# The output of a token tile written in two DMAs instead of one

## The chip, the cores and the metric

The kernel runs on one core of a Trainium2 chip. The metric is the device time of one execution in microseconds (us), as the median of several runs. The core has five instruction queues that matter here: PE (TensorE, matrix multiplications, with the loading of weights shown apart as PEld), DVE (VectorE), ACT (ScalarE), POOL (GpSimd) and SP (SyncE), which in this kernel issues every DMA.

## The reference

Four sequences of 768 tokens, eight heads of 48 elements, so a model width of 384. A delta-rule attention (a serial recurrence over the tokens) is followed by a gated mixer with a causal convolution and by a gated MLP that mixes over tokens:

```python
# attention, per batch and head
k_n = k / (norm(k) + 1e-6)
for t in range(S):
    y[t] = q[t] @ state
    state = state + beta[t] * outer(k_n[t], v[t] - k_n[t] @ state)
# first block
gate = sigmoid(causal_conv5(x, conv_w)); val = x @ w_val
x = (gate * val) @ w_out
# second block
h = gelu_tanh(x @ w_in); u, v = h[..., :512], h[..., 512:]
v_n = (v - mean(v)) / sqrt(var(v) + 1e-6) * g_ln
v_s = w_sg @ v_n + b_sg            # over tokens, 768 x 768
return x + (u * v_s) @ w_out2
```

## The kernel before

The recurrence is worked through in chunks of 64 tokens, 12 per sequence and 48 in all (`seq`, `attend`), with matrices prepared ahead for pairs of chunks (`keys`, `gram`, `base`, `merge`). Its result goes to a DRAM buffer. The two blocks behind it are worked through in token tiles of 256, three per sequence and twelve in all, each in six steps: `front` (load x, convolution, gate), `value`, `hidden`, `gates`, `mix` and `final`. The tiles of one sequence run beside the recurrence of the next; behind the last chunk only tile work is left. Matrices are split into two halves of 16 bits, and each product takes three matmuls (`mm3`).

`final` makes the output of a tile, 384 features by 256 tokens, as three blocks of 128 features. They are taken in two groups, `m0 = 0` with two blocks and `m0 = 2` with one; each group has a PSUM buffer of its own from a ring of three (`bank`). A group's matmuls (nine with `wo` and twelve with `w2` for each block) end in one ACT copy into the tile `o`, of 128x512 or 128x256 elements. Before the change, one DMA then writes the whole of `o` to DRAM (line 998). `o` shares a ring of two buffers (tag `a`) with the tile `a` of `front`, so a `front` that gets its buffer waits until the output DMA has read it.

No instruction is issued when its line runs. Each call is put on record by `Program.add`; `in_order` then lays all of them out in one list with a planner: it gives each operation a planned cost, and a priority that is the weighted cost of the longest chain of operations behind it, divided by the longest chain of all, plus a constant for some stages (lines 119 to 126). The weight of a DMA is 1.949, and its planned time contains its bytes / 250,000 per us. Each engine gets its instructions in the order of the planned times and works through them in that order; SP's list of DMAs is one of these. The planner also lets SP hold when eight DMAs have not landed.

Of the kernel before, what the change touches and what calls it, by code (L numbers as in the profile page):

```python
# [346 lines left out]
def kernel(  # L347
# [17 lines left out]
    nc = Program(tc)  # L365
    P, B, NC, PR, E = kn_in.shape
# [8 lines left out]
    TT = 256  # L375
# [93 lines left out]
    def mm3(ps, a, b, start, stop):  # L469
        for i, (x, y) in enumerate(((0, 0), (0, 1), (1, 0))):  # L470
            nc.tensor.matmul(out=ps, lhsT=a[x], rhs=b[y], start=start and i == 0, stop=stop and i == 2)
# [379 lines left out]
    def wsl(nm, k, cols):  # L851
        return wt[nm][:, 0, k, cols], wt[nm][:, 1, k, cols]
# [5 lines left out]
    def bank():  # L858
        return ps_m.tile([P, 2, TT], F32, name="ps_mlp", tag="m")

    def pairs(n):
        return [(i, min(2, n - i)) for i in range(0, n, 2)]
# [121 lines left out]
    def final(b, tt):  # L984
        gvh = kept.pop(("gv", b, tt))
        gts = [kept.pop(("gt", b, tt, d0)) for d0, _ in pairs(KF)]
        o = mp.tile([P, KD, TT], F32, name="o", tag="a", bufs=2)
        for m0, n in pairs(KD):
            ps = bank()
            for m in range(n):  # L990
                cols = slice((m0 + m) * 128, (m0 + m + 1) * 128)
                for k in range(KD):
                    mm3(ps[:, m], wsl("wo", k, cols), (gvh[:, 0, k], gvh[:, 1, k]), k == 0, False)
                for d in range(KF):
                    mm3(ps[:, m], wsl("w2", d, cols), (gts[d // 2][:, 0, d % 2], gts[d // 2][:, 1, d % 2]),
                        False, d == KF - 1)
            nc.scalar.activation(out=o[:, m0:m0 + n], in_=ps[:, 0:n], func=AF.Copy, scale=1.0 / (SGT * SW2))
        nc.sync.dma_start(out=out[b].rearrange("(k p) t -> p k t", p=P)[:, :, tt * TT:(tt + 1) * TT], in_=o)

# [3 lines left out]
    def add_order(add):  # L1005
        for tt in range(NTT):
            for f in (front, value, hidden):
                add(f, 0, tt)
        for b in range(B):
            nx = b + 1 if b + 1 < B else None  # L1010

            def nxt(f, tt):
                if nx is not None:
                    add(f, nx, tt)

            last = NTT - 1
            nxt(front, 0)
            for tt in range(NTT):
                add(gates, b, tt)
                if tt == 0:  # L1020
                    nxt(value, 0)
                else:
                    add(final, b, tt - 1)
                add(mix, b, tt, 0)
                if tt == 1:
                    nxt(hidden, 0)
                add(mix, b, tt, 2)
            nxt(front, 1)
            nxt(value, 1)
            add(final, b, last)  # L1030
            nxt(front, 2)
            nxt(value, 2)
            nxt(hidden, 1)
            nxt(hidden, 2)
# [96 lines left out]
```

## Time and profile before

| | |
|---|---|
| median of 3 runs | 700.64 us (699.04 to 838.62) |
| profiled execution | 701.2 us |
| its span, first to last instruction | 699.5 us |
| mean granted TensorE clock | 0.912 |
| instructions | 22,383 |
| bytes moved by DMA | 94.42 MB |

The profile is of one execution. Its span is the time from the first to the last instruction on the core; the profiled execution took 1.7 us longer than that. Busy times are sums over instructions of an engine. A granted clock of 1.00 is TensorE at full speed.

### The profile page before, as it was taken

What the parts mean: (1) busy time and instruction counts of PE and PEld (TensorE: products, weight loads), DVE (VectorE), ACT (ScalarE), POOL (GpSimd) and SP (SyncE); (2) the same over time, 40 slices, a digit from 0 to 9 for tenths busy, and PEclk for the clock granted to TensorE, in tenths of its full rate; (3) what the DMA queues carried; (4) which work ended last, traced back from release to release, by engine and by line L of the source; (5) the groups of instructions that cost most, each with busy time, mean ns of one, the idle gap of its engine ahead of it and who ended that gap; (6) DMA issues with size and microseconds to landing.
All of it is one profiled execution on the core that took longest, in us unless ns stands there. A gap on an engine that the chain in (4) does not pass through costs nothing.

```text
span 699.5 us, 22383 instructions
## 1 busy us (share of the span) xinstructions
PE 555.3 (79%) x9183; PEld 459.1 (66%) x9183; DVE 563.7 (81%) x1536; ACT 377.5 (54%) x857; POOL 195.3 (28%) x189
## 2 busy tenths in 40 slices
PE   0615736656696498899989998899999999998897
PEld 0503315645575377688778867797977887776786
DVE  8899999997787889989998999899979746563321
ACT  5644646656567756686455767344667533433111
POOL 4625350246214462433402322002412100102000
PEclk9999866655599599999999999999999999999999
DMA  6643405897788968599668964677674754210121
GB/s 203 165 136 126 147 11 125 181 197 142 150 177 166 238 140 173 111 187 252 137 117 178 235 132 85 144 127 156 147 158 89 150 98 111 86 48 1 53 76 46
DMA packets 327639, 94.42 MB, mean 135 GB/s; under 512 B 274545, under 2 KB 316913, under 8 KB 327537
## 3 DMA queue, kind: packets, MB, share of 16 engines
q1 hardware_dynamic: 327536, 93.00, 59.9%
q8 instruction: 72, 1.18, 0.7%
q14 instruction: 31, 0.25, 0.1%
HBM read 51.81 MB, written 23.33 MB: 107 GB/s over the span
## 4 chain that ended last, share of the span: by engine, by line
DVE 37%; PE 26%; DMA 15%; ACT 10%; issue 6%; SPq 3%; POOL 2%; POOLq 0%; ACTq 0%; DVEq 0%
PE ps_mlp L109 20%; DVE X L109 5%; DVE tmp L109 4%; DVE wst L109 3%; SPq L109 3%; DVE a L109 3%; DMA wg<-wgd 2%; PE ps_y L109 2%; ACT v L109 2%; DVE ps_mlp L109 2%; DMA ws<-wh 2%; DMA m1p<-gx 2%; DVE wh L109 2%; DMA kf<-in_kn 2%; DMA bs<-in_b_sg 2%
## 5 line engine op out<-in xcount | busy, mean ns | idle before, releaser
L109 PE MATMUL ps_mlp<-wg,vnh 128*128 128x256 f16 x864 | 104.5, 273 | 5.6 <-DVE ps_mlp L109 1.6
L109 PEld LDWEIGHTS <-kj 112*128 112x128 f16 (+1 forms) x1632 | 75.3, 101 | 38.1 <-issue 29.0
L109 PEld LDWEIGHTS <-vnh 128*128 128x128 f16 x864 | 82.4, 98 | 19.4 <-issue 3.7
L109 PEld LDWEIGHTS <-kc 64*64 64x64 f16 x1920 | 47.0, 130 | 56.0 <-DVE kc L109 21.7
L109 DVE TENSOR_TENSOR X<-X,tmp 128x30 f32<-128x30 f32 (+9 forms) x180 | 67.5, 375 | 1.7
L109 DVE TENSOR_TENSOR tmp<-X 128x30 f32<-128x30 f32 (+9 forms) x180 | 65.6, 365 | 1.7
L109 PE MATMUL ps_mlp<-gth,w 128*128 128x256 f16 x432 | 60.2, 272 | 0.0
L109 PE MATMUL ps_mlp<-gvh,wi 128*128 128x256 f16 x432 | 57.8, 276 | 2.1 <-ACT u L109 1.1
L109 PE MATMUL ps_mlp<-wi,gvh 128*128 128x512 f16 x216 | 57.6, 379 | 1.9 <-ACT a L109 1.1
L109 PEld LDWEIGHTS <-ws 112*128 112x128 f16 (+1 forms) x1104 | 48.5, 102 | 14.0 <-issue 10.7
L109 PEld LDWEIGHTS <-m1p 128*128 128x128 f16 x1152 | 45.6, 99 | 17.5 <-issue 12.8
L109 DVE SCALAR_TENSOR_TENSOR ps_mlp<-ps_mlp,gl,bs 128x256 f32<-128x256 f32 x48 | 22.7, 488 | 41.8 <-PE ps_mlp L109 41.4
L109 DVE SCALAR_TENSOR_TENSOR a<-x,cw,a 128x256 f32<-128x256 f32 x108 | 54.4, 543 | 0.6 <-ACT a L109 0.5
L109 POOL TENSOR_TENSOR vnh<-v,vnh 128x512 f16<-128x512 f32 x24 | 28.0, 1182 | 89.0 <-ACT vnh L109 89.0
L109 PE MATMUL ps_mlp<-gvh,wo 128*128 128x256 f16 x324 | 49.0, 274 | 4.8 <-ACT u L109 3.0
L109 PE MATMUL ps_mlp<-xh,wv 128*128 128x256 f16 x324 | 51.2, 272 | 0.3 <-ACT o L109 0.3
L109 PEld LDWEIGHTS <-wo 128*128 128x128 f16 x342 | 31.6, 100 | 26.8 <-ACT wo L109 11.1
L109 PE MATMUL ps_y<-mh,ws 128*128 128x64 f16 x576 | 45.7, 199 | 4.4 <-DMA ws<-wh 3.0
L109 PE MATMUL pk<-i,kc 64*64 64x64 f16 x704 | 23.0, 216 | 32.8 <-DVE kc L109 19.4
L109 PE MATMUL ps_y<-qh,ws 112*128 112x64 f16 x528 | 42.7, 198 | 5.4 <-DVE mh L109 5.0
L109 PEld LDWEIGHTS <-wi 128*128 128x128 f16 x432 | 41.0, 98 | 8.3 <-issue 2.8
L109 POOL TENSOR_TENSOR xh<-x,xh 128x780 f16<-128x780 f32 x12 | 20.3, 1690 | 85.4 <-ACT xh L109 81.8
(148 smaller groups left out, 1391.4 us busy)
## 6 DMA issues: line engine op xcount, KB each, us to landing
keys_d<-kc SPq DMA_DIRECT2D x22, 512.0 KB, 4.5
ws<-wh SPq DMA_DIRECT2D x88, 128.0 KB, 3.8
kj<-keys_d SPq DMA_DIRECT2D x44, 256.0 KB, 4.5
wg<-wgd SPq DMA_DIRECT2D x12, 768.0 KB, 5.7
qf<-in_qt SPq DMA_DIRECT2D x24, 224.0 KB, 4.0
kf<-in_kn SPq DMA_DIRECT2D x12, 384.0 KB, 4.4
vf<-in_vn SPq DMA_DIRECT2D x24, 192.0 KB, 3.9
xd<-ys SPq DMA_DIRECT2D x48, 96.0 KB, 2.7
```

Of the source, the lines that this page charges most:

```text
L109: op.call()
```

## The change

The DMA moves into the loop over the two groups. Each group's copy is followed by a DMA of its part of `o`: 256 KB for `m0 = 0`, 128 KB for `m0 = 2`. Everything else in the source stays.

```diff
@@ def final(b, tt):
             nc.scalar.activation(out=o[:, m0:m0 + n], in_=ps[:, 0:n], func=AF.Copy, scale=1.0 / (SGT * SW2))
-        nc.sync.dma_start(out=out[b].rearrange("(k p) t -> p k t", p=P)[:, :, tt * TT:(tt + 1) * TT], in_=o)
+            nc.sync.dma_start(out=out[b].rearrange("(k p) t -> p k t", p=P)[:, m0:m0 + n, tt * TT:(tt + 1) * TT],
+                              in_=o[:, m0:m0 + n])
```

## Rows read from the trace of the kernel before

**Rows 1.** The page: engine, busy us, share of the span, instructions.

```profile
PE 555.3 (79%) x9183; PEld 459.1 (66%) x9183; DVE 563.7 (81%) x1536; ACT 377.5 (54%) x857; POOL 195.3 (28%) x189
```

**Rows 2.** Busy time by stage: stretch, its length, then engines, clock, DMA share.

```profile
0.00:327.00 327.00, 209.10 (x4287) 168.57 (x4288) 293.05 (x777) 201.95 (x460) 132.89 (x142) 0.82 0.69 160
327.00:555.00 228.00, 215.15 (x3535) 181.21 (x3533) 207.11 (x594) 131.00 (x304) 52.32 (x39) 1.00 0.71 141
555.00:611.00 56.00, 53.67 (x729) 46.63 (x726) 31.97 (x86) 22.77 (x54) 3.94 (x3) 1.00 0.45 103
611.00:643.00 32.00, 28.75 (x216) 20.72 (x216) 17.34 (x57) 13.25 (x25) 6.19 (x5) 1.00 0.12 37
643.00:668.30 25.30, 22.41 (x188) 19.14 (x188) 7.28 (x14) 3.37 (x6) 0.00 (x0) 0.93 0.13 37
668.30:673.70 5.40, 4.62 (x42) 3.75 (x41) 1.88 (x3) 1.97 (x4) 0.00 (x0) 1.00 0.74 214
673.70:695.20 21.50, 21.50 (x196) 19.07 (x196) 5.05 (x9) 2.30 (x6) 0.00 (x0) 1.00 0.08 27
695.20:699.50 4.30, 0.10 (x1) 0.00 (x0) 0.00 (x0) 0.84 (x2) 0.00 (x0) 0.92 0.26 91
```

**Rows 3.** The page: the chain that ended last, by engine.

```profile
DVE 37%; PE 26%; DMA 15%; ACT 10%; issue 6%; SPq 3%; POOL 2%; POOLq 0%; ACTq 0%; DVEq 0%
```

**Rows 4.** Groups by line and form: count, busy us, mean ns, idle before.

```profile
L109 ACT ACTIVATE o<-ps_mlp 128x512 f32<-128x512 f32 x12 | 7.1, 593 | 22.9 <-PE ps_mlp L109 22.9
L109 ACT ACTIVATE o<-ps_mlp 128x256 f32<-128x256 f32 x12 | 4.5, 378 | 3.4 <-PE ps_mlp L109 3.4
```

**Rows 5.** DMA issues: count, KB each, median us from issue to landing.

```profile
xd<-ys SPq DMA_DIRECT2D x48, 96.0 KB, 2.7
out_x<-o SPq DMA_DIRECT2D x12, 384.0 KB, 3.0
```

**Rows 6.** Timeline of ACT, one tile's two copies: start us, us, instruction.

```profile
395.48 0.37 ACT L109 ACTIVATE o<-ps_mlp 128x256 f32<-128x256 f32 x1
...
408.50 0.60 ACT L109 ACTIVATE o<-ps_mlp 128x512 f32<-128x512 f32 x1 [0.16 <-PE ps_mlp L109]
```

**Rows 7.** The chain that ended last, its last pieces: start us, us, what.

```profile
695.17 0.60 ACT o L109
695.77 0.28 ACTq L1127
```

**Rows 8.** Timeline of all engines at the end of the span.

```profile
695.17 0.87 ACT L109 ACTIVATE o<-ps_mlp 128x512 f32<-128x512 f32 x2 [5.44 <-PE ps_mlp L109]
696.07 0.37 SPq L109 DMA_DIRECT2D out_x<-o  x1
```

**Rows 9.** DMA from 690 to 700 us, 40 slices, and the last issue.

```profile
GB/s 336 360 352 262 4 0 0 0 0 0 0 0 0 0 0 0 0 0 0 0 0 0 0 0 0 0 0 29 328 352 336 356 172 0 0 0 0 0 0 0
...
out_x<-o SPq DMA_DIRECT2D x1, 384.0 KB, 2.5
```

**Rows 10.** Timeline of SP's queue around the output at 409 us.

```profile
409.12 0.40 SPq L109 DMA_DIRECT2D out_x<-o  x1
409.99 2.85 SPq L109 DMA_DIRECT2D tbd<-tah  x3
412.94 1.82 SPq L109 DMA_DIRECT2D kj<-keys_d  x2
```

**Rows 11.** The chain that ended last, seen from the stretch 300 to 420 us.

```profile
409.12 4.07 DMA out_x<-o
```

**Rows 12.** Waits from 405 to 420 us: total us, times, longest.

```profile
ACT a L109 <- DMA out_x<-o: 0.4, 1, 0.4
```

**Rows 13.** Waits of SP's queue from 327 to 555 us.

```profile
SPq L109 <- ACT o L109: 3.0, 1, 3.0
```

## The prediction

> **What bounds the kernel now.** I began with the busy shares [rows 1]: PE and DVE are busy for 79% and 81% of the span, so neither bounds all of it, and the span has to be cut into stages. The stage table [rows 2] does that. Up to 327 us DVE is busy for 293.05 of 327 us at a mean granted clock of 0.82; no tile's output is written there. From 327 to 555 us PE (215.15 of 228) and DVE (207.11 of 228) are both nearly full and the DMA engines are busy for 0.71 of the time: recurrence, matrices of the next set and the token tiles run side by side. From 555 us on PE is what counts: 53.67 of 56, 28.75 of 32, 22.41 of 25.3, 4.62 of 5.4 and 21.5 of 21.5 us. The last 4.3 us hold almost no PE work: they are the last copy and the last output DMA. The chain of waits [rows 3] says the same by engine: DVE 37%, PE 26%, DMA 15%, and SP's queue, into which the new DMAs go, only 3%.
>
> The output path itself: twelve tiles, each with one copy of 128x512 (593 ns) and one of 128x256 (378 ns) [rows 4] and one DMA of 384 KB that lands after a median of 3.0 us [rows 5]. The two copies of a tile are not always neighbours. In one tile the narrow one starts at 395.48 and the wide one at 408.50 us [rows 6]; the list puts whichever matmuls it likes first. In the last tile they are neighbours: the chain's end shows the wide copy at 695.17 for 0.60 us and then the other [rows 7], the two together take 0.87 us and the DMA is issued at 696.07 [rows 8].
>
> **The change part by part.** It removes twelve DMAs of 384 KB and adds twelve of 256 KB and twelve of 128 KB; no byte, matmul or copy is added. I make the sum against the profiled execution, 701.2 us (span 699.5 plus 1.7 around it), which lies 0.56 us above the median of 700.64.
>
> *The tail.* In the last tile, 1.15 us of the DMA's time is data: the DMA slices [rows 9] are full from about 696.75 on, at 328 to 356 GB/s, mean 343, and 393,216 bytes / 343 GB/s = 1.15 us; it lands 2.5 us after its issue. Half sizes: 256 KB take 0.76, 128 KB take 0.38 us. What is gained depends on which half ends last. (a) If the copies stay together as now, the first half is issued at 695.80, the second 0.40 us later (one issue is 372 to 400 ns, rows 8 and 10), at 696.20; with the same 0.68 us from issue to data as now, the data ends at 696.48 + 1.15 = 697.63 in place of 697.90: 0.27 us gained. (b) If the list finishes the wide group first, the wide copy and its DMA lie beside the narrow group's matmuls; after PE's end come only the narrow copy (0.38 for 0.87, 0.49 gained) and 128 KB of data (0.76 gained): 1.25 us. (c) If the wide group ends last, 0.27 + 0.39 = 0.66. The worst is a second issue that is 0.13 us later than today's single one with nothing gained in the data. I take (b), -1.25, since the list's priorities contain the size of the DMA behind an operation: by lines 119 to 122 a 256 KB DMA is worth 1.949 x 131,072 / 250,000 = 1.02 more than a 128 KB one, some twelve matmuls of priority, and so the wide group goes ahead. Bounds -1.25 to +0.13.
>
> The Trainium skill (DMA: Bandwidth & Descriptors, Anatomy of one DMA) gives a DMA of the gpsimd path about 2.0 us plus bytes / 436 GB/s; by that figure the data term of (b) would be 0.60 in place of 0.76, an estimate that leaves the sum within 0.2 us.
>
> *The buffer behind it.* o and front's a share a ring of two buffers, so a later front waits until the output has been read. That wait shows once: the chain of a middle stretch runs through the output DMA that was issued at 409.12 and took 4.07 us [rows 11], and ACT lost 0.4 us to it [rows 12]. With the last DMA smaller the buffer can come free earlier, by at most the 0.4 that was lost: 0 to -0.4, I take -0.2. Then ACT is held by DVE, as before.
>
> *SP's time.* Twelve more issues at the 0.40 us of [rows 10]: 4.8 us of SP, six of them beside the recurrence (2.4 us). An issue costs something only if the transfer queued behind it is awaited; SP's queue is 3% of the chain [rows 3], so I take +0.5 between 0.1 (3% of 4.8, rounded) and 4.8. After 585 us nothing hurries behind it; before, the cover is SP's spare time, and without it all 4.8 would show.
>
> *The added wait on SP.* SP works through its list in order, so the first half's issue waits for its copy with everything behind it. Between 327 and 555 us SP waited once for a copy of o, 3.0 us [rows 13], in six output DMAs (the tiles of the first two sequences): queued behind were the pieces of tbd and the kj of the next step [rows 10], for which the recurrence's matmuls wait. Six new such issues: one more wait of that kind is likely, and as kj is fetched ahead I let 0.5 of 3.0 through; bounds 0 and 3.0.
>
> *The new order.* This is the largest term, and the one that no row of before shows. The whole program is one list, laid out by a planner from its own costs. The new operations move planned times from the first output on, and sizes change the weighted chains; where the longest one ends in the last output, all priorities are rescaled by a thousandth or so and ties flip from the start. So I expect the instructions of all engines in another order in many places, with the same work. What that can win is PE's uncovered time in the stretches behind the recurrence, 611 to 673.7 us, where PE alone decides and another filling can help: 3.25 + 2.89 + 0.78 = 6.92 us [rows 2]. Before that a hole of PE lies beside a nearly full DVE and I don't count on filling it. What it can lose is of the size of what a mixed stretch loses today, 12.85 us in 327 to 555 [rows 2]. Between -6.92 and +12.85 the middle is +3.0, and I take that; no row favours one end.
>
> Sum: 701.2 - 1.25 - 0.2 + 0.5 + 0.5 + 3.0 = 703.75 in the profile's terms, less 0.56 against the median: 703.2 us, 0.4% over before.
>
> **The rivals.** *Slower: outputs block SP's list.* If the first halves are planned where ACT really comes late, each of the six in the busy stretch holds SP as at 409 us: 3.0 + 0.40 = 3.4 us, and what is held is tbd, kj and ws, on which the serial recurrence waits. Six times 3.4 is 20.4 us: 700.6 + 20.4 = 721. It decides from the fifth that passes whole (17 us, 2.4%). For it: DMA is 15% of the chain, SP's queue is packed back to back around the outputs [rows 10]. Against: only one of the six present outputs was waited for there, and kj is fetched a step ahead. Chance 0.11, with the part of the order term that goes beyond its bound.
>
> *Faster: the new order fills PE's holes.* All of PE's uncovered time from 327 to 695.2 us is 12.85 + 2.33 + 3.25 + 2.89 + 0.78 = 22.1 us; to pass 2% it would have to fill 14 of them, with the tail 13. Time about 686. Against: PE's holes before 611 us lie beside a DVE that is busy for over nine tenths up to 555. Chance 0.02.
>
> *Every DMA pays its fixed time.* If the part of a transfer that doesn't depend on its size stood on the path, the twelve added DMAs would cost twelve times the 2.7 us that a 96 KB DMA takes to land [rows 5]: 32 us, 733. Against: SP goes on to the next issue 0.87 us after the output's at 409.12 [rows 10], long before its landing at 413.2, and nobody but a late front waits for an output. Chance 0.01. The Trainium skill (the same page, Rules for kernel authors) speaks for this rival: it wants many small transfers coalesced into one large one. The rows of 96 KB and 384 KB, 2.7 and 3.0 us, agree that size matters little to landing; they don't show that landing is on the path.
>
> *The change does nothing but split.* If the order stays, the time is 700.6 with 0.3 to 1.3 us off: 699.4 to 700.4, inside the forecast's range. Chance 0.08, since the planner uses the sizes.
>
> **How the numbers follow.** A measurement of this kernel can tell about 2%, 14 us, from no change. The forecast (0.78) and the bare split (0.08) lie within it, 0.86; slower by over 2% are the first rival and the third, 0.12; faster has 0.02. For the range, all terms at their low ends give 700.64 - 1.25 - 0.4 + 0.1 - 6.92 = 691.8. Upwards, the order term at its end gives 703.2 + 9.85 = 713; with the other costs half way to their ends (2.1 and 1.2) 716.4. All ends at once (721) is the slower rival, which I leave out: 692 to 716.
>
> **What would show it.** Twelve output DMAs of 256 and twelve of 128 KB, issued at about 0.4 us each, one right behind each copy. At the end: a wide copy that starts over 1 us before PE's end, one narrow copy after it, and some 0.5 us less from PE's end to the last issue. No row in the waits in which SP holds for a copy of o longer than 3 us before 555 us. If another wait (wg, kj, X) has grown in the chain while the bytes and busy times stay as they are, it is the order. The prediction is wrong if the two traces have the same order of instructions (then less than 700.6), or if the recurrence's stretch up to 585 us has grown by over 10 us behind SP's waits.

## The result: one per cent slower

Median 707.34 us (703.53 to 713.44) against 700.66 before; the ratio is 1.0101, with a 95% interval of 1.0055 to 1.0148. That is inside the 2% that the prediction called no change and inside its range of 692 to 716, but it is clear of noise, and the cause was open: the prediction had put +3.0 us on the new order and +1.0 on SP. A ratio, here and below, is worked out from the single executions, the few slow ones left out, and need not be the quotient of the two medians.

The page of the changed kernel (the profiled execution took 706.63 us), busy shares and chain by engine, against [rows 1] and [rows 3]:

```profile
span 704.8 us, 22396 instructions
...
PE 560.8 (80%) x9183; PEld 462.3 (66%) x9183; DVE 567.7 (81%) x1536; ACT 378.4 (54%) x857; POOL 194.6 (28%) x189
...
DVE 32%; PE 32%; DMA 12%; ACT 8%; issue 7%; SPq 6%; POOL 3%; POOLq 0%; ACTq 0%; DVEq 0%
```

The counts of PE, DVE, ACT and POOL are those of before: no work was added. PE is busy for 5.5 us longer with the same 9,183 matmuls, so some of them ran slower; SP's queue has gone from 3% to 6% of the chain, which looks like the prediction's first rival. Its output DMAs stand against those of [rows 5]: two thirds and one third of the bytes land after a median of 2.3 and 2.4 us, where the whole took 3.0.

```profile
out_x<-o SPq DMA_DIRECT2D x12, 256.0 KB, 2.3
...
out_x<-o SPq DMA_DIRECT2D x12, 128.0 KB, 2.4
```

The stage table shows where the time went. Its borders are the issues of the same `wg` load in both kernels (to about a microsecond), so each row holds about the same work. First the changed kernel, then the kernel before; columns as in [rows 2]:

```profile
327.00:474.00 147.00, 138.42 (x2378) 116.85 (x2376) 141.34 (x403) 83.09 (x196) 31.78 (x25) 1.00 0.69 140
474.00:565.00 91.00, 83.39 (x1219) 68.45 (x1216) 71.31 (x200) 49.33 (x112) 19.79 (x14) 0.96 0.65 127
565.00:616.00 51.00, 50.26 (x667) 43.70 (x665) 28.05 (x76) 21.33 (x49) 3.93 (x3) 1.00 0.44 106
616.00:704.80 88.80, 77.54 (x656) 63.40 (x654) 33.97 (x86) 22.93 (x42) 6.20 (x5) 1.00 0.17 50
```

```profile
327.00:474.00 147.00, 137.12 (x2367) 116.00 (x2365) 137.56 (x398) 83.32 (x197) 31.39 (x25) 1.00 0.71 143
474.00:555.00 81.00, 78.02 (x1171) 65.21 (x1168) 69.55 (x197) 47.68 (x108) 20.93 (x14) 1.00 0.70 136
555.00:608.50 53.50, 52.13 (x717) 45.41 (x714) 29.55 (x81) 21.58 (x52) 3.94 (x3) 1.00 0.45 105
608.50:699.50 91.00, 78.92 (x654) 63.90 (x651) 33.96 (x86) 22.92 (x42) 6.19 (x5) 0.98 0.16 49
```

Up to 474 us nothing is lost. The next stretch takes 91 us in place of 81, with a PE clock of 0.96 in place of 1.00. Behind it 2.5 and 2.2 us come back. The instruction lists agree: PE's list is the same up to its 4,667th matmul, at about 351 us, and from there it differs in some 1,900 places; the first difference in SP's list is the first output, at 344 us.

Inside that stretch, the recurrence's copy of its state on ACT marks each chunk. Two neighbouring ones, changed kernel first:

```profile
482.07 0.33 ACT L109 ACTIVATE wh<-ps_state 112x192 f16<-112x192 f32 x1 [3.03 <-PE ps_state L109]
...
499.36 0.33 ACT L109 ACTIVATE wh<-ps_state 112x192 f16<-112x192 f32 x1 [1.34 <-PE ps_state L109]
```

```profile
481.15 0.33 ACT L109 ACTIVATE wh<-ps_state 112x192 f16<-112x192 f32 x1 [2.67 <-PE ps_state L109]
...
492.88 0.35 ACT L109 ACTIVATE wh<-ps_state 112x192 f16<-112x192 f32 x1
```

17.3 us in place of 11.7: 5.6 us in one chunk. The changed kernel's copies of the state are 0.9 us late ahead of this chunk, 6.5 us behind it, 4.2 and 2.2 at the next two, and 8.2 at the third. That third copy stands behind a cast on ACT that waits for its load, a second place at which time is lost:

```profile
535.21 0.85 ACT L109 ACTIVATE xh<-x 128x780 f16<-128x780 f32 x1 [2.76 <-DMA x<-xd]
```

Here are DVE, then POOL, then PE of the changed kernel in the chunk of 17.3 us:

```profile
481.64 0.20 DVE L109 TENSOR_TENSOR X<-X,tmp 128x30 f32<-128x30 f32 x1
481.75 4.31 DVE L109 SCALAR_TENSOR_TENSOR a<-x,cw,a 128x256 f32<-128x256 f32 x4
485.98 0.48 DVE L109 SCALAR_TENSOR_TENSOR ps_mlp<-ps_mlp,gl,bs 128x256 f32<-128x256 f32 x1
```

```profile
481.92 1.43 POOL L109 TENSOR_SCALAR_AFFINE_SELECT X<-X 128x1024 f32<-128x1024 f32 x1 [18.48 <-DVE X L109]
483.41 0.16 POOL L109 MEMSET X<- 128x32 f32 x1
483.65 2.12 POOL L109 TENSOR_TENSOR X<-X,bt 128x1024 f32<-128x1024 f32 x1
```

```profile
486.51 4.00 PE L109 MATMUL ps_mlp<-wg,vnh 128*128 128x256 f16 x18 [3.80 <-DVE ps_mlp L109]
```

And the same place in the kernel before:

```profile
483.08 0.20 DVE L109 TENSOR_TENSOR X<-X,tmp 128x30 f32<-128x30 f32 x1
483.19 0.42 DVE L109 SCALAR_TENSOR_TENSOR qh<-qf,qh 112x256 f16<-112x256 f32 x1
483.52 1.67 DVE L109 SCALAR_TENSOR_TENSOR a<-x,cw,a 128x256 f32<-128x256 f32 x4
```

```profile
483.36 2.96 POOL L109 TENSOR_SCALAR_AFFINE_SELECT X<-X 128x1024 f32<-128x1024 f32 x1 [27.36 <-DVE X L109]
```

```profile
482.86 2.12 PE L109 MATMUL ps_mlp<-wg,vnh 128*128 128x256 f16 x18 [1.13 <-DVE ps_mlp L109]
```

Read it from DVE. Four convolution steps of a later tile take 4.31 us in the new list and 1.67 in the old, and POOL's work on X starts beside them in both. In the new list DVE is held up, in the old one POOL is (2.96 for 1.43). Behind the four stands the mix's step, for which PE waits 3.80 us. PE then works at half speed: its next 18 matmuls take 4.00 us in place of 2.12. The stage table of the changed kernel around that stop gives the clock:

```profile
481.00:482.50 1.50, 1.46 (x34) 1.25 (x33) 1.50 (x6) 0.43 (x2) 0.58 (x1) 1.00 0.74 117
482.50:486.50 4.00, 0.21 (x1) 0.00 (x0) 4.00 (x5) 0.50 (x2) 3.13 (x3) 0.90 1.04 218
486.50:493.00 6.50, 6.49 (x37) 3.94 (x37) 4.31 (x12) 1.09 (x3) 0.00 (x0) 0.54 0.43 71
493.00:500.00 7.00, 7.00 (x107) 6.40 (x106) 5.67 (x13) 5.00 (x8) 2.74 (x1) 1.00 0.17 57
```

The granted clock is 1.00 before the stop and 0.54 in the 6.5 us behind it, so near the lower of its two levels (1.2 of 2.4 GHz); from 493 us it is back. The kernel before keeps 1.00 in all four stretches.

So there were two theories to tell apart. *Order*: the DMAs cost nothing, the re-laid list does. *Issue or wait*: SP's added issues, or its added waits for a copy, cost the time.

### The profile page after: what moved, and what is told of

Its sections match the earlier page's. It is cut to its first block, busy times and chain, and to the rows that moved or that the text cites. A ratio compares the mean times of both kernels' runs of the same rounds, so it can differ in the third digit from the quotient of the medians.

```text
span 704.8 us, 22396 instructions
## 1 busy us (share of the span) xinstructions
PE 560.8 (80%) x9183; PEld 462.3 (66%) x9183; DVE 567.7 (81%) x1536; ACT 378.4 (54%) x857; POOL 194.6 (28%) x189
## 3 DMA queue, kind: packets, MB, share of 16 engines
q8 instruction: 72, 1.18, 0.7%
## 4 chain that ended last, share of the span: by engine, by line
DVE 32%; PE 32%; DMA 12%; ACT 8%; issue 7%; SPq 6%; POOL 3%; POOLq 0%; ACTq 0%; DVEq 0%
PE ps_mlp L109 24%; SPq L109 6%; DVE X L109 4%; DVE a L109 4%; PE ps_y L109 3%; DVE tmp L109 3%; DVE wst L109 3%; DVE ps_mlp L109 2%; DMA bs<-in_b_sg 2%; DMA x<-xd 2%; PE ps_q L109 2%; DMA wg<-wgd 2%; ACT v L109 2%; DMA wst<-in_w_out 2%; DVE wh L109 1%
## 5 line engine op out<-in xcount | busy, mean ns | idle before, releaser
L109 PE MATMUL ps_mlp<-wg,vnh 128*128 128x256 f16 x864 | 106.4, 276 | 12.8 <-DVE ps_mlp L109 6.5
L109 PEld LDWEIGHTS <-kj 112*128 112x128 f16 (+1 forms) x1632 | 77.2, 102 | 38.0 <-issue 28.7
L109 PE MATMUL ps_mlp<-gvh,wi 128*128 128x256 f16 x432 | 56.0, 272 | 3.0 <-ACT v L109 1.6
L109 DVE SCALAR_TENSOR_TENSOR a<-x,cw,a 128x256 f32<-128x256 f32 x108 | 56.5, 570 | 1.5 <-ACT a L109 1.4
L109 PE MATMUL ps_mlp<-gvh,wo 128*128 128x256 f16 x324 | 45.7, 272 | 4.6 <-ACT u L109 2.6
```

The lines of the kernel that those rows point to most:

```text
L109: op.call()
```

## The experiments

All ratios are to the kernel before on the same chip, with a 95% interval.

| kernel | what differs | median us | ratio |
|---|---|---|---|
| e1 | old list, two DMAs at the old place | 703.66 | 1.0040 [1.0013, 1.0067] |
| e2 | new list, one DMA | 710.00 | 1.0108 [1.0066, 1.0149] |
| e3 | old list, each half behind its copy | 701.49 | 1.0009 [0.9979, 1.0039] |
| e4 | old list, six DMAs | 708.32 | 1.0112 [1.0070, 1.0153] |
| e5 | new list, convolution steps moved | 701.20 | 1.0016 [0.9996, 1.0036] |
| e6 | new list, cast moved | 708.04 | 1.0113 [1.0086, 1.0141] |
| e7 | new list, both moved | 702.42 | 1.0008 [0.9983, 1.0032] |
| e8 | last tile alone in two DMAs | 699.44 | 0.9982 [0.9950, 1.0014] |
| e9 | new list, mix's step moved alone | 705.64 | 1.0066 [1.0032, 1.0099] |
| e10 | old list, one query step moved | 703.98 | 1.0054 [1.0024, 1.0084] |
| n1 | another list, one DMA | 701.89 | 1.0007 [0.9978, 1.0037] |
| n3 | another list, one DMA | 706.19 | 1.0065 [1.0035, 1.0095] |

**Lists and DMAs apart (e1 to e4).** The planner can be shown one thing and the chip given another: an operation goes on record with the sizes that the planner is to see, and its call issues what is wanted.

```diff
 # e1: the planner sees one DMA; its call issues two
-        nc.sync.dma_start(out=dst, in_=o)
+        def parts():
+            for part in (slice(0, 2), slice(2, 3)):
+                tc.nc.sync.dma_start(out=dst[:, part], in_=o[:, part])
+        nc.add("sync", "dma_start", parts, dict(out=dst, in_=o))
 # e2: the planner sees two; the later call issues the whole
+            nc.add("sync", "dma_start", partial(whole, dst, o, seen), dict(out=dst[:, m0:m0 + n], in_=o[:, m0:m0 + n]))
 # e3, in trace(): the first half goes out once its copy is planned to end, the second at the old place
             for op in ops:
+                while early and early[0][0] <= op.start:
+                    early.pop(0)[2]()
                 op.call()
 # e4: as e1, one block of features and half the tokens at a time
+            for k in range(KD):
+                for h in range(2):
```

> The planner sees the one DMA of before, so all engines keep the list of before; only at the place of the output DMA in SP's list two DMAs (256 and 128 KB) are issued one behind the other. Theory 'order' (the 1% comes from the new list of instructions, not from the DMAs): 699 to 702 us, no change. Rival 'issue' (the twelve more issues on SP cost the time): 705 to 709 us.

> The planner sees the two DMAs of the changed kernel, so PE, DVE, ACT and POOL have the lists of the changed kernel; but one DMA of 384 KB is issued, at the place of the later of the two, and nothing at the other. Theory 'order': 705 to 709 us, 0.6 to 1.3% over before, though the output is written as before. Rivals 'issue' and 'wait' (the cost lies in the added DMAs or in SP's added waits): 699 to 702 us.

> The list of before on PE, DVE, ACT and POOL; of SP's list only the output DMAs change: each half is issued behind its own copy, the first as soon as its copy is planned to be done, the second at the old place. This is the change without its new order. Theory 'order': 699 to 702 us. Rival 'wait' (SP's new holds for the first copy delay tbd, kj and ws): 704 to 710 us, with more time of SP spent in waits for copies of o before 555 us.

> The list of before, with six DMAs of 64 KB (one block of features, half the tokens each, rows of 512 bytes) at the place of each output DMA: 60 more issues than before. Doubles the cost of 'issue' fivefold: at 6.7 us for twelve it expects 730 to 735 us, and 24 us more of SP's time. Theory 'order': under 705 us, only what 30 more issues beside the recurrence let through.

The pair that decides is e2 and e3. The changed kernel's list without its DMAs (e2) costs 1.08%, as much as the change; its DMAs without its list (e3) cost 0.09%, not to be told from nothing. In e3 SP waited for a copy of o once between 327 and 555 us, for 1.0 us, less than before [rows 13]:

```profile
SPq L115 <- ACT o L116: 1.0, 1, 1.0
```

So *wait* falls. *Issue* has a small part: e4's 60 added DMAs cost 1.12% of 700.35, 7.8 us or 0.13 us each, so twelve would cost 1.6 us at that rate; what of it is the issue and what the smaller transfer was not told apart. In "doubles the cost fivefold" the expectation counts 60 against 12. e4 missed the under 705 that *order* had expected, by 3 us, and was over 21 us below what *issue* had. e1 stays unclear: 0.4% is more than its twelve issues give by e4's price, and in its profiled execution, the slowest of its twelve, the state's copy that before starts at 304.66 us starts at 307.79, so 3.1 us of its excess lie ahead of the first output, where the lists are the same.

**Which part of the list (e5 to e7, e9).** The changed kernel, with single operations moved in the finished list; in each move no operation is carried past one that needs it.

```diff
 # in trace(), on the changed kernel's list
         ops = self.in_order()
+        ops = self.move(ops, convs, last)   # e5: the four steps behind the mix's, the state's and tbd's step
+        ops = self.move(ops, [cast], wh)    # e6: the cast xh behind the copy of the state
+        # e7: both moves;  e9: ops = self.move(ops, convs, mix), behind the mix's step alone
```

> The changed kernel with one edit of its list: four of DVE's convolution steps, which in its trace take 4.31 us beside POOL's work on X at 482 us while the mix's step and the recurrence's step stand behind them, are moved behind those steps. Theory 'two places' (the new list loses its time at two places, this one and the cast at 532 us): chunk 16 of the recurrence comes 3 to 6 us earlier, 702 to 705 us in all. Rival 'spread' (these places only show a loss that sits in the whole list): no change, 706 to 709 us.

> The changed kernel with another edit of its list: one ACT cast (xh of the first tile of the last sequence), which in its trace waits for its load of x while the recurrence's copy of the state stands behind it for some 2.8 us, is moved behind that copy. Theory 'two places': the state's copy comes 3 to 6 us earlier, 702 to 705 us in all. Rival 'spread': 706 to 709 us.

> Both moves of the two kernels above in the changed kernel's list. Theory 'two places': the loss is gone and the gain of the last tile is left, 698 to 702 us. Rival 'spread': 705 us and more.

> The changed kernel with the four convolution steps moved behind the mix's DVE step alone; they still stand ahead of the recurrence's steps (the state's copy and tbd). Theory 'PE's stop' (the loss is PE standing still for 3.8 us behind the mix's step and then running at half its clock): most of it is gone, 700 to 703 us. Rival 'recurrence' (the loss is the recurrence's DVE step that stands behind the four): 705 to 709 us.

e5 takes the loss away with four DVE steps moved by six places: 1.0016, with 1 in its interval, some 0.8% below the changed kernel and lower than either theory had. e6 takes none (1.0113, as its rival *spread* had): in its trace the cast no longer stands ahead of the state's copy and that chunk is 2.5 us shorter, the next one is 0.8 longer, and over its six executions nothing is gained. e7 is e5 again, 0.4 us above what *two places* had. So *two places* falls; one decides. By the state's copies e5 is 4.7 us ahead of the kernel before at 518 us and level with it at 540: the new list wins and loses time at other places too, and without this one they come out even. The rows of e5, DVE, POOL and PE, at that place:

```profile
480.42 0.48 DVE L137 SCALAR_TENSOR_TENSOR ps_mlp<-ps_mlp,gl,bs 128x256 f32<-128x256 f32 x1
...
482.42 2.02 DVE L137 SCALAR_TENSOR_TENSOR a<-x,cw,a 128x256 f32<-128x256 f32 x5
```

```profile
482.15 4.07 POOL L137 TENSOR_TENSOR X<-X,bt 128x1024 f32<-128x1024 f32 x1
```

```profile
481.21 2.13 PE L137 MATMUL ps_mlp<-wg,vnh 128*128 128x256 f16 x18
```

The steps now take 0.40 us each, POOL is held up (4.07 us for 2.12), PE waits for nothing and keeps its clock. e9 asks what share each half of the harm has. There the mix's step goes ahead, and nothing else:

```profile
484.10 0.48 DVE L147 SCALAR_TENSOR_TENSOR ps_mlp<-ps_mlp,gl,bs 128x256 f32<-128x256 f32 x1
484.49 4.14 DVE L147 SCALAR_TENSOR_TENSOR a<-x,cw,a 128x256 f32<-128x256 f32 x4
488.55 0.68 DVE L147 BATCH_NORM_STATS2 st<-v 128x6 f32<-128x512 f32 x1
489.15 0.34 DVE L147 SCALAR_TENSOR_TENSOR wh<-ps_state,wh 112x192 f16<-112x192 f32 x1
```

```profile
484.89 2.13 PE L147 MATMUL ps_mlp<-wg,vnh 128*128 128x256 f16 x18
...
489.54 0.26 PE L147 MATMUL ps_q<-wh,kj 112*128 112x48 f16 x4 [2.32 <-DVE wh L147]
```

The mix's 18 matmuls are neither held nor slowed. PE stops later, for 2.32 us, until the recurrence's step is done, and its granted clock stays at 1.00. Yet 1.0066 is left, inside what the rival *recurrence* had: the four steps still take 4.14 us and the recurrence's step on its state stands behind them. By the points of the ratios the mix's stop and the slow clock are worth 0.35% (1.0101 to 1.0066) and the recurrence's hold 0.50% (1.0066 to e5's 1.0016). The intervals of e9 and of the changed kernel overlap, so the first share is not shown to differ from nothing. The traces have it the other way round: the chunk takes 17.3 us in the changed kernel, 13.2 in e9 and 10.8 in e5. How the loss divides stays open.

**The harm put into the old list (e10).** One operation moved, PE's, ACT's, POOL's and SP's lists as before.

```diff
-X<-X,tmp   qh<-qf,qh   a x4   ps_mlp     (DVE's list before)
+qh<-qf,qh   X<-X,tmp   a x4   ps_mlp
```

> The list of before with one DVE step (the query's lower half, qh) moved ahead of the last step on X, so that the four convolution steps follow X at once, as in the changed kernel. Theory 'pairing' (which of DVE and POOL holds the other up is decided by what stands on DVE when POOL's work on X begins): the four take about 4.3 us in place of 1.67, and the time grows by 1 to 4 us, 702 to 705. Rival: they stay at 1.7 us and the time is that of before, 699 to 702.

```profile
483.84 0.20 DVE L124 TENSOR_TENSOR X<-X,tmp 128x30 f32<-128x30 f32 x1
483.96 4.30 DVE L124 SCALAR_TENSOR_TENSOR a<-x,cw,a 128x256 f32<-128x256 f32 x4
488.18 0.48 DVE L124 SCALAR_TENSOR_TENSOR ps_mlp<-ps_mlp,gl,bs 128x256 f32<-128x256 f32 x1
```

```profile
484.12 1.44 POOL L124 TENSOR_SCALAR_AFFINE_SELECT X<-X 128x1024 f32<-128x1024 f32 x1 [28.88 <-DVE X L124]
```

4.30 us in place of 1.67, as *pairing* had it, and 0.54% of time; the chunk takes 14.3 us in place of 11.7. The pairing is shown from both sides: taken out of the new list the loss goes, put into the old one a loss comes. The traces of e2 and e6, which keep the new list here, have 4.30 us too. In e10 the mix's first step stands ahead of the four and its matmuls are not slowed (2.13 us); what comes later is the mix's second step and the recurrence's.

The Trainium skill (SBUF — State Buffer, SBUF: two separate sides) says that DVE and GpSimd have a pair of ports in common, held for a whole instruction by whichever starts first, also by a DVE operation with two SBUF inputs against a GpSimd operation that reads SBUF, and that the other stands still. The convolution step and the query's step have two such inputs, and the rows agree that one of the two engines is held up at each meeting. Singly, the four steps of the changed kernel take 0.47, 1.47, 0.47 and 2.13 us. The two long ones:

```profile
482.14 1.47 DVE L109 SCALAR_TENSOR_TENSOR a<-x,cw,a 128x256 f32<-128x256 f32 x1
...
483.93 2.13 DVE L109 SCALAR_TENSOR_TENSOR a<-x,cw,a 128x256 f32<-128x256 f32 x1
```

The first ends about 0.3 us behind POOL's select, the second about 0.3 us behind POOL's addition (`X<-X,bt`), so DVE stood still for one POOL instruction each time and got a step through between the two. In the old list it isn't a matter of one instruction: all four steps take 0.48 us, and POOL's select, 2.96 us long, ends 1.1 us behind the last of them. Nor do the starts in the trace decide: e5's POOL addition is shown from 482.15, 0.27 us ahead of its first step, and is held all the same. Why POOL gets in between two DVE steps in one list and not in the other is not shown by these runs.

The planner reckons with such a hold (`held` in `in_order`): a POOL operation that comes while DVE has a step with two SBUF inputs waits until DVE's string of them is over. So in both of its plans the four steps run through and POOL's select waits behind them. The chip did that in the old list and not in the new one.

**The tail alone (e8), and two other lists (n1, n3).**

```diff
 # e8, in final's loop; all other tiles keep their one DMA
+            if (b, tt) == (B - 1, NTT - 1):
+                nc.sync.dma_start(... m0:m0 + n ..., in_=o[:, m0:m0 + n])
 # n1, n3: one DMA per tile; only the planner's cost of issuing it grows, by 0.3 and 0.6 us
-    return 0.68 if onchip or n > 4 * row else 0.48, move, False
+    more = 0.3 if out.tensor.name == "out_x" else 0.0
+    return (0.68 if onchip or n > 4 * row else 0.48) + more, move, False
```

> Only the last of the twelve tiles is written in two DMAs, and the planner knows it; the lists of ACT, DVE and POOL are those of before, PE's differs in a few ties and in the last tile, SP's in the last DMA. The prediction's tail term (b): 1.25 us less, 698.5 to 700 us, with one narrow copy and 128 KB after the last matmul. Rival: the copies stay together and at most 0.3 us is gained, or the ties of PE cost it, 700 to 703 us.

> Another list from the same kernel as before: one output DMA per tile as before, only the planner's cost of issuing it is 0.3 us higher, which changes some 1,900 places of PE's list and none of the work. Its DVE list has no convolution steps between the last step on X and the mix's step. Theory 'place' (only a list with that pairing loses): 698 to 703 us. Rival 'any other list loses': 704 to 710 us.

> As the kernel with 0.3 us, with 0.6 us: a third list, in which single convolution steps stand among others behind the last step on X. Theory 'place': 698 to 704 us. Rival 'any other list loses': 704 to 710 us.

e8's ratio of 0.9982 has 1 in its interval: its point is the prediction's tail term (0.0018 x 701 = 1.3 us), but the measurement can't confirm it. Its ratio is the lowest of the twelve, and no version was shown to beat both kernels. n1 shows that a different list need not lose, and not even one in which DVE is held up:

```profile
485.76 4.56 DVE L109 SCALAR_TENSOR_TENSOR a<-x,cw,a 128x256 f32<-128x256 f32 x5
```

These five steps run beside POOL's next work, and the chunk takes 18.2 us, but that list was 5.4 us ahead of the kernel before when the chunk began, and its whole time is level with it. n3 loses 0.65%, inside what the rival had, without the four-step pairing: by the state's copies it is 2 us early at 506 us and 5 us late at 528. So *place* is too narrow: other lists lose at other places, and n3's was not followed up.

## Why the prediction held, and where it didn't

*The tail* (-1.25 us) was right in mechanism and size. In the changed kernel the list finished the wide group first, as the priorities by size had said (that the sizes did it was not tested apart). The timeline of ACT, the chain's end and the last DMAs:

```profile
700.17 0.60 ACT L109 ACTIVATE o<-ps_mlp 128x512 f32<-128x512 f32 x1 [4.13 <-PE ps_mlp L109]
701.65 0.38 ACT L109 ACTIVATE o<-ps_mlp 128x256 f32<-128x256 f32 x1 [0.88 <-PE ps_mlp L109]
```

```profile
699.00 2.63 PE ps_mlp L109 x24
701.63 0.02 issue
701.65 0.38 ACT o L109
```

```profile
out_x<-o SPq DMA_DIRECT2D x2, 128.0 KB, 1.7
out_x<-o SPq DMA_DIRECT2D x1, 256.0 KB, 2.1
```

The wide copy starts 1.48 us ahead of the narrow one. From the start of the first copy behind PE's end to the end of the span it is 704.8 - 701.65 = 3.15 us, against 699.5 - 695.17 = 4.33 before [rows 7]: 1.18 us gained, 1.25 forecast. The narrow DMA lands after 1.7 us where the whole took 2.5 [rows 9].

*The two terms on SP* (+0.5 each, with 4.8 and 3.0 as far ends) were right to stay small: e3 puts the two DMAs without the new list at +0.09%, -1.5 to +2.7 us. Little of the tail's gain is in that, since e3's last two copies stay together: from the first copy's start to the end are 4.17 us for 4.33. The price per DMA from e4, 0.13 us, makes 1.6 us of the twelve, between the low end and the far one. The rival *outputs block SP's list* is refuted for this list: by e2 (the loss without the DMAs), by e3's single wait of 1.0 us, and by the changed kernel's own trace, in which SP waits for no copy of o between 327 and 555 us. That SP's share of the chain doubled was no sign of it.

*The buffer behind o* (-0.2) was not measured apart.

*The new order* (+3.0, from -6.92 to +12.85) was named the largest and least certain term, and the runs agree on both: e2 against one, 1.08%, is 7.6 us, and the change less e3, 0.92%, is 6.4 us. That is inside its bounds and over twice the size; with it the sum gives 706.6 to 707.8 us in place of 703.2. The sign was luck: +3.0 was the middle between two bounds, not the outcome of a mechanism, and n1's list shows that another order can cost nothing. Two parts of its reasoning failed. First, "ties flip from the start": the list is the same up to the first output. Second, I sized it by PE's uncovered time, as if orders won or lost by filling holes. What lost was an operation made longer by its neighbour on another engine (4.31 for 1.67 us on DVE), which no sum of idle time contains.

*That every DMA pays its fixed time* fell with e3 and e4: at 2.7 us each, e4's 60 would have cost 162 us.

Two figures of the working are off, without consequence: the low ends add up to 692.2, not 691.8, and in [rows 9] the data flow from 697.0 us on rather than 696.75, which cancels in the differences.

## What to carry to other kernels

Where a planner lays out the whole program, an edit of one line is two edits: what the line does, and the new list. Time them apart, by showing the planner the one and giving the chip the other, before explaining anything. When a new list loses, set the milestones of a serial chain side by side, find the step where the gap opens, and look there for operations whose own duration has changed. Then take the suspect out of the new list and put it into the old one: other places of the list will look as guilty and be worth nothing. A gain of a microsecond at the tail is worth having only if the list ahead of it is kept.

## What the runs showed of the hardware

An operation's duration can depend on what stands just ahead of it on its own engine, beside the same work of another. The same four DVE steps with two SBUF inputs took 1.67 us or 4.30 beside the same POOL work, decided in e10 by the place of one step of 0.42 us ahead of them. And a stop of PE of 3.80 us cost PE more than itself: the 18 matmuls behind it took 4.00 us for 2.12, at a granted clock of 0.54. Behind e9's stop of 2.32 us the clock stayed at 1.00.
